# First loads, warm-up and one PSUM bank: six small changes at the start of a gated attention and FFN kernel

## The chip, the cores and the metric

The kernel runs on one core of one Trainium2 chip. The metric is the device time of one execution in microseconds (us); most kernels here were executed six times, and a change in time is judged against executions of the kernel before on the same chip in the same rounds. One execution of each kernel was traced. Its span (first to last instruction of the program) is about 1.25 us shorter than its device time. The traced execution of the kernel before took 288.19 us, less than any of the three executions that the prediction starts from.

## The reference

x is 2048 tokens of width 640 (bf16). Branch A is linear attention with 32 heads of width 20; branch B is a GEGLU feed-forward net of width 1728; a sigmoid gate mixes them.

```python
g = _sigmoid((x * gate_w).sum(-1, keepdims=True))
# A: q, k, v = x @ wqkv per head; pq = q @ w_phi, pk = k @ w_phi
#    phi = concat(softmax(p), softmax(-p)); kv = phi_k^T v; z = sum phi_k
#    a = ((phi_q @ kv) / (phi_q . z + 1e-6)) @ wo
# B: b = (gelu(x @ w_gate) * (x @ w_up)) @ w_down
return g * a + (1 - g) * b
```

## The kernel before

Everything that the change touches lies in the first 30 us. Loads are issued in program order, each engine on its own queue; a turned load (`dma_start_transpose`) brings x or a weight with its axes exchanged.

```python
    def loads(self):
        ...                                   # x: 4 tiles of 128 tokens in the first block
        sc.op("pool", ... memset gz ...)
        xload("sp", 0)                        # tiles 0, 1 (320 KB) on SyncE
        xload("act", 2)                       # tiles 2, 3 (320 KB) on ScalarE
        sc.dma("act", ... wphi_sb ...)        # 640 rows of 40 bytes
        for kt in range(KD):                  # V weight, five pieces of 160 KB
            sc.dma("sp", lambda e: e.dma_start(self.w3[:, kt, 0:D], w3[:, kt, 2 * D:3 * D]), writes=[("wv", kt)])
        sc.dma("act", ... gate_w into gz ...)
        xturn(4, 2)                           # tiles 4, 5 turned     } all on SyncE
        wload(self.wkT, D, "wkT")             # key weight turned     }
        xturn(6, 2)                           # tiles 6, 7 turned     }
        wload(self.wqT, 0, "wqT")             # query weight turned   }
        xturn(8, 4)
        xturn(12, 4)
        ...                                   # FFN weights, then masks on GpSimd

    def x_transpose(self, t, b, ek):          # five 128x128 transposes on TensorE into bank b,
        ...                                   # then one copy by ScalarE ("a") or VectorE ("d")

    def pq(self, b, i, n):                    # one query chunk
        bank = 6 + n % 2
        ...                                   # 5 matmuls, then exp(+) and exp(-) on ScalarE from that bank

    def attention_state(self):
        sc.op("dve", lambda e: e.memset(self.zero[:, :], 0.0), writes=["zero"])
        warm(7)                               # 7 matmuls of 512 columns on zeros, to wake the array
        xt(0, 6, "d"); xt(1, 7, "a"); xt(2, 2, "d"); xt(3, 3, "a")
        ...                                   # V projection of tiles 0-3, weight piece by weight piece
        self.v_early(4, 6); self.v_early(5, 0)          # needs tiles 4, 5
        f(0, "k", (2, 3), "d"); f(1, "k", (4, 5), "a")  # folds w_phi into the key weight: needs wkT
        self.v_early(6, 6)                              # needs tile 6
        ...                                             # f(0, "q", ...) needs wqT
        self.k_early(3, 0)                              # banks 0, 1
        self.k_norm(1)
        self.pq(0, 1, 1); self.pq(0, 0, 0); self.pq(0, 3, 3)   # banks 7, 6, 7
        self.gram(0)                                    # Gram product of tile 0
        ...
```

The softmax here doesn't subtract the row's maximum and nothing guards it: scores larger than these inputs give would overflow.

## Time and profile before

| | |
|---|---|
| device time | 288.81 us (288.63 to 288.95, 3 executions) |
| TensorE busy | 281.2 of 286.9 us |
| TensorE idle that the change aims at | the waits of the first 28.3 us |
| last wait of TensorE that matters | third query chunk, 0.34 us, until 28.34 us |

What it does not show is SyncE's queue, from the timeline of the first 12 us; columns are start, duration, engine ("SPq" is SyncE's queue of DMA issues), line, operation, operands and count.

```profile
0.79 0.41 SPq L217 DMA_DIRECT2D xtok<-in_A_x_dram  x1
1.27 2.30 SPq L234 DMA_DIRECT2D w<-in_A_wqkv_dram  x5
3.62 1.44 SPq L225 DMA_TRANSPOSE xT<-in_A_x_dram  x1
5.10 4.58 SPq L221 DMA_TRANSPOSE wkT<-in_A_wqkv_dram  x1
9.72 1.41 SPq L225 DMA_TRANSPOSE xT<-in_A_x_dram  x1
```

The durations are those of the issue, not of the transfer. The key weight (L221) holds the queue for 4.58 us, and tiles 6 and 7 can only be issued after it.

### The profile page before, as it was taken

What the parts mean: (1) busy time and instruction counts of PE and PEld (TensorE: products, weight loads), DVE (VectorE), ACT (ScalarE), POOL (GpSimd) and SP (SyncE); (2) the same over time, 40 slices, a digit from 0 to 9 for tenths busy, and PEclk for the clock granted to TensorE, in tenths of its full rate; (3) what the DMA queues carried; (4) which work ended last, traced back from release to release, by engine and by line L of the source; (5) the groups of instructions that cost most, each with busy time, mean ns of one, the idle gap of its engine ahead of it and who ended that gap; (6) DMA issues with size and microseconds to landing.
All of it is one profiled execution on the core that took longest, in us unless ns stands there. A gap on an engine that the chain in (4) does not pass through costs nothing.

```text
span 286.9 us, 7006 instructions
## 1 busy us (share of the span) xinstructions
PE 281.2 (98%) x3017; PEld 185.5 (65%) x3032; DVE 174.7 (61%) x353; ACT 105.0 (37%) x199; POOL 5.3 (2%) x36
## 2 busy tenths in 40 slices
PE   8999999999999999999999999999999999999996
PEld 3666689999994444444444444445777777777785
DVE  3248999999977553567242334225883883883801
ACT  3367887677663322322323223221112112112111
POOL 7000000000000000000000000000000000000000
PEclk9999999999999999999999999999999999999999
DMA  8999995000002000011000000000232333422221
GB/s 226 206 187 247 367 367 174 0 2 2 2 0 48 0 0 0 3 24 23 2 0 0 0 2 0 0 2 0 25 94 62 35 48 92 49 49 85 56 72 48
DMA packets 36937, 18.67 MB, mean 65 GB/s; under 512 B 28970, under 2 KB 36394, under 8 KB 36906
## 3 DMA queue, kind: packets, MB, share of 16 engines
q1 hardware_dynamic: 36096, 17.86, 26.1%
q8 instruction: 24, 0.39, 0.6%
q10 hardware_dynamic: 810, 0.35, 0.5%
q14 instruction: 7, 0.06, 0.1%
HBM read 9.04 MB, written 2.62 MB: 41 GB/s over the span
## 4 chain that ended last, share of the span: by engine, by line
PE 93%; SPq 3%; DMA 2%; ACT 1%; issue 1%; ACTq 0%
PE ps L352 60%; PE ps L714 28%; PE ps L658 2%; DMA xT<-in_A_x_dram 2%; PE ps L450 2%; SPq L221 2%; PE ps L332 1%; SPq L234 1%; SPq L225 1%; ACT Ek L414 0%; ACT Eq L519 0%; SPq L217 0%; ACT outsb L727 0%; ACT gcol L417 0%; ACTq L42 0%
## 5 line engine op out<-in xcount | busy, mean ns | idle before, releaser
L352 PE MATMUL ps<-xT,wg_sb 128*128 128x512 bf16 (+1 forms) x265 | 63.8, 379 | 0.4 <-issue 0.2
L352 PE MATMUL ps<-xT,wu_sb 128*128 128x512 bf16 (+1 forms) x263 | 63.3, 379 | 0.5 <-DVE hT L632 0.2
L630 ACT ACTIVATE gl<-ps 128x512 bf16<-128x512 f32 x52 | 30.9, 596 | 73.1 <-PE ps L352 68.7
L632 DVE TENSOR_TENSOR hT<-ps,gl 128x512 bf16<-128x512 f32 x39 | 26.7, 690 | 38.6 <-PE ps L352 38.5
L714 PE MATMUL ps<-wd_sb,hT 64*128 64x320 bf16 x648 | 49.5, 296 | 0.0
L352 PEld LDWEIGHTS ps<-xT,wu_sb 128*128 128x128 bf16 (+1 forms) x270 | 26.5, 99 | 29.8 <-DVE hT L632 0.5
L352 PEld LDWEIGHTS ps<-xT,wg_sb 128*128 128x128 bf16 (+1 forms) x270 | 26.2, 99 | 29.0 <-ACT gl L630 0.2
L352 PE MATMUL ps<-w,xT 128*64 128x512 bf16 (+6 forms) x398 | 41.6, 325 | 0.4 <-DMA xT<-in_A_x_dram 0.2
L727 ACT ACTIVATE outsb<-ps,Gm 128x320 bf16<-128x320 f32 (+2 forms) x31 | 14.5, 515 | 72.4 <-PE ps L714 72.4
L352 PEld LDWEIGHTS ps<-w,xT 128*64 128x64 bf16 (+1 forms) x400 | 35.8, 107 | 5.1 <-DMA xT<-in_A_x_dram 0.4
L714 PEld LDWEIGHTS ps<-wd_sb,hT 64*128 64x128 bf16 x648 | 31.0, 94 | 12.1 <-issue 0.4
L714 PE MATMUL ps<-wo_sb,goT 64*128 64x320 bf16 (+2 forms) x340 | 27.8, 288 | 0.0
L352 PE MATMUL ps<-xT,wq 128*64 128x512 bf16 (+1 forms) x184 | 26.1, 381 | 0.4 <-ACT Eq L519 0.3
L434 DVE TENSOR_TENSOR Ek<-Ek,Dk 128x640 bf16<-128x640 bf16 x32 | 25.0, 822 | 0.6
L685 DVE TENSOR_TENSOR O<-ps,RH 128x640 bf16<-128x640 f32 x32 | 24.8, 816 | 0.0
L425 DVE TENSOR_REDUCE Dk<-Ek 128x64 f32<-128x1280 bf16 x16 | 23.7, 1479 | 0.1
L519 ACT ACTIVATE Eq<-ps 128x512 bf16<-128x512 f32 x40 | 21.7, 605 | 1.1 <-PE ps L352 0.8
L414 ACT ACTIVATE Ek<-ps 128x640 bf16<-128x640 f32 x32 | 20.7, 703 | 3.6 <-PE ps L352 3.6
L632 DVE TENSOR_TENSOR xT<-ps,gl 128x512 bf16<-128x512 f32 x13 | 9.0, 691 | 18.2 <-PE ps L352 18.2
L714 PEld LDWEIGHTS ps<-wo_sb,goT 64*128 64x128 bf16 x340 | 16.1, 94 | 5.4
L352 PEld LDWEIGHTS ps<-xT,wq 128*64 128x64 bf16 (+1 forms) x185 | 15.3, 109 | 3.4 <-ACT Eq L519 0.8
L714 PE MATMUL ps<-wd_sb,xT 64*128 64x320 bf16 (+2 forms) x270 | 16.7, 269 | 0.0
(69 smaller groups left out, 173.2 us busy)
## 6 DMA issues: line engine op xcount, KB each, us to landing
out_dram<-outsb SPq DMA_DIRECT2D x7, 320.0 KB, 2.3
wd_sb<-in_B_w_down_dram SPq DMA_DIRECT2D x1, 2080.0 KB, 14.3
wg_sb<-in_B_w_gate_dram SPq DMA_DIRECT2D x1, 1120.0 KB, 5.7
wu_sb<-in_B_w_up_dram SPq DMA_DIRECT2D x1, 1120.0 KB, 8.2
wg_sb<-in_B_w_gate_dram SPq DMA_DIRECT2D x1, 960.0 KB, 9.8
wu_sb<-in_B_w_up_dram SPq DMA_DIRECT2D x1, 960.0 KB, 10.4
w<-in_A_wqkv_dram SPq DMA_DIRECT2D x5, 160.0 KB, 4.7
wo_sb<-in_A_wo_dram SPq DMA_DIRECT2D x1, 800.0 KB, 9.7
```

The costliest lines, as they stand in the source:

```text
L221: sc.dma("sp", lambda e: e.dma_start_transpose(T[:, :, :], self.wqkv[:, c0:c0 + D]), writes=[key])
L352: self.sc.op("pe", lambda e: e.matmul(self.ps[a:z, bank * 512 + c0:bank * 512 + c0 + n], lhs[:, a:z], rhs, start=first, stop=fin), reads=r ...
L414: self.sc.op("act", lambda e, s=s, scale=scale: e.activation(self.Ek[:, se, s, :], self.ps[:, o:o + self.D], AF.Exp, scale=scale), reads=[ ...
L425: sc.op("dve", lambda e: e.tensor_reduce(self.Dk[:, se, 0, :].rearrange("p (s h) -> p s h", h=H), self.Ek[:, se, :, :].rearrange("p s (h d ...
L434: sc.op("dve", lambda e, v=v, r=r: e.tensor_tensor(v, v, r, ALU.mult), reads=[("Rk", se)], writes=[("Ek", se, s)])
L450: sc.op("pe", lambda e: e.matmul(self.ps[a:a + 64, b * 512 + c:b * 512 + c + 2 * nf], va[:, lo:lo + 64], self.Ek[:, se, :, f0:f0 + nf], st ...
L519: sc.op("act", lambda e, s=s, scale=scale: e.activation(self.Eq[:, s, i, b * self.BT:(b + 1) * self.BT], self.bank(bank), AF.Exp, scale=sc ...
L630: sc.op("act", lambda e: e.activation(self.gl[:, slot, :], self.bank(banks[0]), AF.Gelu_apprx_tanh), reads=[("ps", banks[0])], writes=[("g ...
L632: sc.op("dve", lambda e: e.tensor_tensor(hT, self.bank(banks[1]), self.gl[:, slot, :], ALU.mult), reads=[("ps", banks[1]), ("gl", slot)], ...
L685: dve(lambda e, o=o, f=f, s=s: e.tensor_tensor(o, V[s][:, :, :, 0:DH], f, ALU.mult), rb + [key(6 + s)], [("O", s, sl)], guard=old)
L714: sc.op("pe", lambda e: e.matmul(self.bank(bk, w), lhs, rhs, start=opens and x == 0, stop=end and not opens, skip_group_check=True), reads ...
L727: sc.op("act", lambda e: e.activation(dst, self.bank(bk, w), AF.Copy, scale=g), reads=rd, writes=wr)
```

## The change

Two words first. TensorE's array starts "cold" (0.43 us from one 512-column matmul to the next) and is later "warm" (0.22 us). The "head" is everything up to the first query chunk, near 26 us.

The intent of the change: the first half of x should arrive earlier, undisturbed by the second half and by w_phi's many short rows; the warm-up should not wait for a memset; ScalarE's table should be loaded early; tile 3 should not wait for ScalarE's slower copy; and the third query chunk should not wait for bank 7.

```diff
@@ alloc @@
-        self.zero = T("zero", [P, 512], BF16)
         self.gz = T("gz", [P, P], BF16)
         self.gcol = T("gcol", [P, NT], F32)
         self.gtmp = T("gtmp", [P, NT], F32)
@@ -225,11 +224,17 @@
             sc.dma("sp", lambda e: e.dma_start_transpose(self.xT[:, :, a:z], self.x[a:z, :]),
                    writes=[("xT", k) for k in range(t, t + n)])
         sc.op("pool", lambda e: e.memset(self.gz[:, :], 0.0), writes=["gz"])
+        sc.op("act", lambda e: e.activation(self.gtmp[:, 0:1], self.nc.const_aps.tensor(1.0, [P, 1], BF16), AF.Exp),
+              writes=["gtmp"])
+        sc.op("pool", lambda e: e.memset(self.ident[:, :], 0.0), writes=["ident"])
+        sc.op("pool", lambda e: e.affine_select(self.ident[:, :], self.ident[:, :], pattern=[[-1, P]],
+                                                compare_op=ALU.not_equal, fill=1.0, base=0, channel_multiplier=1),
+              writes=["ident"])
         xload("sp", 0)
-        xload("act", 2)
+        xload("sp", 2)
         sc.dma("act", lambda e: e.dma_start(
             self.wphi_sb[:, :, :], self.wphi.rearrange("h d f -> (h d) f").rearrange("(i p) f -> p i f", p=P)),
-            writes=["wphi"])
+            reads=["ident"], writes=["wphi"])
         for kt in range(KD):
             sc.dma("sp", lambda e: e.dma_start(self.w3[:, kt, 0:D], w3[:, kt, 2 * D:3 * D]), writes=[("wv", kt)])
         sc.dma("act", lambda e: e.dma_start(self.gz[0:KD, :], self.gw.rearrange("(k p) -> k p", p=P)), writes=["gz"])
@@ -258,9 +263,6 @@
 
         def pool(fn, writes, reads=()):
             sc.op("pool", fn, reads=reads, writes=writes)
-        pool(lambda e: e.memset(self.ident[:, :], 0.0), ["ident"])
-        pool(lambda e: e.affine_select(self.ident[:, :], self.ident[:, :], pattern=[[-1, P]],
-                                       compare_op=ALU.not_equal, fill=1.0, base=0, channel_multiplier=1), ["ident"])
         for i in range(KD):
             n = self.HHI[i] - self.HLO[i] + 1
             base = P * i - DH * self.HLO[i]
@@ -509,9 +511,9 @@
                       writes=[("KV", i, r, g)])
                 self.kvk[i, r].append(("KV", i, r, g))
 
-    def pq(self, b, i, n):
-        sc = self.sc
-        bank = 6 + n % 2
+    def pq(self, b, i, n, bank=None):
+        sc = self.sc
+        bank = 6 + n % 2 if bank is None else bank
         for kt in range(self.KD):
             self.mm(bank, 0, 512, self.wq2[:, kt, i * P:(i + 1) * P], self.xT[:, kt, b * self.BT:(b + 1) * self.BT],
                     kt == 0, kt == self.KD - 1, [("xT", t) for t in range(4 * b, 4 * b + 4)] + [("wq2", kt)])
@@ -534,18 +536,15 @@
         NT = self.NT
         order = [(b, i) for b in range(self.NB) for i in range(self.KD)]
         sc = self.sc
-        sc.op("dve", lambda e: e.memset(self.zero[:, :], 0.0), writes=["zero"])
-
-        def warm(n):
-            for i in range(n):
-                sc.op("pe", lambda e: e.matmul(self.bank(0), self.zero[:, 0:P], self.zero[:, :], start=True, stop=True),
-                      reads=["zero"], writes=[("ps", 0)])
+        ones = self.nc.const_aps.tensor(1.0, [P, 512], BF16)
+        for n in (512, 512, 512, 512, 512, 512, 128):
+            sc.op("pe", lambda e: e.matmul(self.bank(0, n), ones[:, 0:P], ones[:, 0:n], start=True, stop=True),
+                  writes=[("ps", 0)])
         vs, ve, xt = self.v_step, self.v_first_evac, self.x_transpose
-        warm(7)
         xt(0, 6, "d")
         xt(1, 7, "a")
         xt(2, 2, "d")
-        xt(3, 3, "a")
+        xt(3, 3, "d")
         for t in range(4):
             vs(t, 0)
         for t in range(4):
@@ -585,7 +584,7 @@
         self.k_norm(1)
         self.pq(0, 1, 1)
         self.pq(0, 0, 0)
-        self.pq(0, 3, 3)
+        self.pq(0, 3, 3, 0)
         self.columns = True
         self.gram(0)
         self.k_norm(2)
```

## The prediction

> **What bounds the kernel now.** I read the page first: busy shares, then the strip of 40 slices.
>
> ```profile
> PE 281.2 (98%) x3017; PEld 185.5 (65%) x3032; DVE 174.7 (61%) x353; ACT 105.0 (37%) x199; POOL 5.3 (2%) x36
> PE   8999999999999999999999999999999999999996
> PEclk9999999999999999999999999999999999999999
> ```
>
> TensorE has work in hand for 281.2 of 286.9 us at the full granted clock, and only the first slice is short of 9 apart from the last. The change takes no matmul out of the stream except seven warm-up ones, of which it puts back six and a quarter. So all it can win is idle time of TensorE, and I listed that next, with the waits by length over the whole span and then the timeline of TensorE and its weight loads in the first 30 us. The rows that show a wait:
>
> ```profile
> 0.92 0.27 DVE L537 MEMSET zero<- 128x256 uint32 x1 [0.92 <-PEq L830]
> 1.24 3.17 PE L541 MATMUL ps<-zero 128*128 128x512 bf16 x7 [1.24 <-DVE zero L537]
> 4.28 1.12 PEld L291 LDWEIGHTS ps<-ident,xtok 128*128 128x128 bf16 x20 [0.78 <-DMA xtok<-in_A_x_dram]
> 5.81 0.39 PEld L364 LDWEIGHTS ps<-w,xT 128*128 128x128 bf16 x4 [0.30 <-ACT xT L297]
> 6.41 3.40 PEld L364 LDWEIGHTS ps<-w,xT 128*128 128x128 bf16 x26 [0.21 <-ACT xT L297]
> 14.80 1.36 PEld L352 LDWEIGHTS ps<-w,xT 128*128 128x128 bf16 x10 [0.36 <-DMA xT<-in_A_x_dram]
> 20.00 0.58 PEld L332 LDWEIGHTS ps<-BD,wqT 128*128 128x128 bf16 x11 [0.21 <-DMA wqT<-in_A_wqkv_dram]
> 28.34 1.25 PE L352 MATMUL ps<-xT,wq 128*128 128x512 bf16 x5 [0.34 <-ACT Eq L519]
> ```
>
> In order: warm-up behind a VectorE memset; transposes behind the load of x; V projection of the first block behind ScalarE's copies of transposed tiles 1 and 3; the V projection of tile 6 behind the turned load of x tiles 6 and 7; the first fold of the query weight behind the turned query weight; and the third query chunk behind ScalarE's exponentials. After 28.34 the same list over the rest of the span has only 0.2 us behind VectorE and 0.2 us of issue. So all that matters happens in the first 28 us, and what shift exists at 28.3 us reaches the end unchanged. Then the chain of waits for the first 40 us, to see which of these count:
>
> ```profile
> 3.62 1.44 SPq L225
> 5.10 4.58 SPq L221
> 9.72 5.04 DMA xT<-in_A_x_dram
> 14.76 0.05 issue
> 14.80 1.53 PE ps L352 x10
> ...
> 25.94 1.30 ACT Ek L414 x2
> 27.24 0.07 ACT gcol L417
> 27.30 0.99 ACT Eq L519 x2
> 28.29 0.05 issue
> 28.34 1.25 PE ps L352 x5
> ```
>
> The chain does not run through x's first load, the warm-up or the copies at all. Up to 14.76 it is SyncE's queue of DMA issues and the landing of x tiles 6 and 7. A saving on TensorE before 14.6 us therefore ends in a longer wait at 14.8, unless that landing comes earlier too. Only the ScalarE piece at 25.94 to 28.29 is on the chain and touched by the change.
>
> **What the Trainium skill says.** (1) "DMA: Bandwidth & Descriptors", Issuing engines are not separate DMA queues: DMAs of ScalarE and SyncE run on the same 16 DMA engines and interleave, and a second issuer saves only issue time. The trace agrees: the two halves of x, issued together at 0.79, landed 3.5 and 3.6 us later, both at about 4.3. (2) The same page, Queues, rings and completion order: each engine goes round the rings that have work, a packet at a time. That is why w_phi, on ScalarE's ring behind its half of x, moved only from about 3.7 us (686 packets of that queue in 3.7 to 4.9). With x gone from this ring it will be served as soon as it is issued, between x's packets. (3) "TensorE: Matmul & The Clock Gate", Part 1: about 3.4 us of activity wakes the array, a 512-column matmul taking 426.7 ns cold, 215.7 warm. The weight loads of the warm-up start at 1.65, 2.07, 2.50, 2.93 and 3.35, 0.43 apart, so cold; the 20 transposes from 4.28 take 1.29 in all, so warm. (4) "ScalarE activation tables: per-element evaluation and per-set limits", What a function is on this engine, puts one table load at 1283 ns; the trace has one of 1283 ns at 2.44 and one at the GELU.
>
> **The change part by part.**
> Warm-up: the memset and its wait go. The other engines start their own work at 0.79, so the first matmul can start near 0.85 rather than 1.24. Six of 0.427 and one of 0.107 are 2.67 us, ending near 3.5 rather than 4.23.
> x in turn: by the DMA windows the engines moved 0.65 MB by about 3.7 us, and both halves landed near 4.3, 0.55 us after. Served first, half one (0.33 MB) has moved by about 2.75 and lands near 3.3; tiles 0 and 1 are turned from about 3.5, perhaps still cold (10 x 0.107 = 1.07 at most), to 4.2 or 4.6. Half two, slowed a little by w_phi's packets, lands at 4.3 to 4.5, and tiles 2 and 3 take 10 x 0.057 = 0.57: V projection from about 5.1 rather than 5.42. The first piece of the V weight landed near 1.27 + 3.7 = 5.0, so earlier is not to be had. Gain there, 0.3.
> Tile 3's copy on VectorE: 492 ns there against 700 on ScalarE, and tile 1 is copied about 0.7 earlier, so the two waits of 0.30 and 0.21 mostly go. In the matmul row they are 4.56 us of stream against 16 x 0.27 = 4.34, so the gain is 0.2.
> Early exponential: moves the 1283 ns table load from 2.44 to 0.8. It was over at 3.72, before the first copy at 5.06: worth 0.
> w_phi: its wait for the identity (ready at 1.65) moves the issue from 1.24 to about 1.7. VectorE needs it at 5.74 and TensorE only at 13.8, so even a landing at 6 costs 0.
> Sum so far: TensorE is ready for tile 6 at 14.62 - 0.5 = 14.1. But tile 6 landed at 14.76. So this 0.5 is worth 0 unless the landing moves by d.
> The landing: SyncE has one more issue of 0.41 plus a gap, 0.46 in all, ahead of the five weight pieces and everything after. If issue set the pace, d = +0.46. The DMA windows say otherwise for most of it:
>
> ```profile
> 2.75:3.75 1.00, 1.00 (x3) 0.30 (x2) 0.00 (x0) 0.97 (x1) 0.77 (x6) 1.00 0.99 389
> 4.50:6.50 2.00, 2.00 (x27) 1.39 (x25) 1.66 (x6) 1.30 (x2) 1.72 (x14) 1.00 1.09 334
> 7.50:11.00 3.50, 3.50 (x28) 2.18 (x27) 0.47 (x2) 0.57 (x2) 0.00 (x0) 1.00 1.24 275
> ```
>
> The last two columns are the share of the 16 engines and GB/s: they are full from 2 to 6.5 us and again from 7.5 to 11, so bytes queue up behind the issues. The turned key weight took 4.58 us to issue for 640 rows, where 256 rows took 1.44: in proportion 3.60, so about 1.0 us of it was waiting for room. That slack is more than 0.46, and the bytes ahead are the same as before. I take d = 0, with +0.46 possible. The query weight, issued 5.87 us long, follows the same rule.
> Free bank: the third chunk waited for bank 7 until 28.29. Bank 0 was last read by the key exponentials of tile 3, done at 27.24, while TensorE gets there at 28.00. So the whole 0.34 of matmul idle goes. The next reader, the Gram product of tile 0, then comes at 29.19 rather than 29.52; VectorE is done with that tile at 28.99, so there is room, but only 0.2. ScalarE idles 0.33 in each later round, so it keeps up.
> Sum: 0 (head) + d (0) - 0.34 = -0.34, hence about 288.81 - 0.34 = 288.47; I say 288.45.
>
> **The rivals.**
> First, SyncE's issue order is the bound up to 14.8: each landing comes 0.46 later, the bank returns 0.34, and the time is 288.81 + 0.46 - 0.34 = 288.93. For it speaks the chain, which goes through these issues; against it the 1.0 us of slack in the key weight's issue. About one in five.
> Second, the landing comes earlier, because x no longer alternates with w_phi and V pieces, or a pause that the windows show at 6.5 to 7.5 (98 GB/s) shrinks. Then up to 0.5 of TensorE's head becomes real: 288.81 - 0.34 - 0.4 = about 288.1. About one in five.
> Third, the bank's gain is lost again at the Gram product or in bank 6, which the fourth chunk still needs. VectorE is busy from 25 to 50 us almost without a gap (3.58 us a tile against TensorE's 3.82), so lost TensorE time can't hide there but margins grow by 0.2 a tile. Then 288.8. One in ten.
> Fourth, the short warm-up ends before x arrives and the clock wakes late. Cold V projections would be bounded by the 0.5 of slack for the first microsecond; beyond that the time would rise to about 289. One in twenty.
>
> **Range and chances.** The likely outcomes run from 288.1 to 288.9, and the runs before scatter by 0.16 each way. I predict 288.45, and 287.95 to 288.9 for eight in ten. 2% is 5.8 us, while all idle of TensorE in the first 30 us is about 2 us by the windows (8.76, 9.64, 5.85 and 3.76 us busy in the stretches ending at 10, 20, 25.9 and 30): faster by over 2% gets 0.01, slower 0.01, within 0.98.
>
> **What would show it.** Warm-up matmuls from about 0.85 without a memset; the first transposes waiting near 3.5 and a second wait for x near 4.3; no row of the V projection waiting for ScalarE; the wait for x tiles 6 and 7 grown from 0.36 to about 0.9 with the matmul still at 14.8 (14.3 would be the second rival, 15.2 the first); no wait for ScalarE at the third query chunk; the Gram product of tile 0 about 0.3 earlier. A third chunk that still waits, or a new wait of the Gram product for VectorE, would prove the bank's term wrong.

## The result, and the profile after

Ratios here are the mean time of one kernel's fast executions over the mean of the other's from the same rounds, so not quite the ratio of the medians.

| kernel | median us | lowest to highest | ratio to before, 95% interval |
|---|---|---|---|
| before, same rounds | 288.72 | 288.10 to 288.95 (6) | |
| changed | 287.94 | 287.54 to 288.57 (6) | 0.9979 [0.9963, 0.9994] |
| before, a later call, other chip | 288.48 | 287.68 to 288.92 (11) | |
| changed, that call | 288.09 | 287.71 to 289.35 (6) | 0.9995 [0.9975, 1.0014] |

The means differ by 0.62 us in the first call and 0.11 in the second, 0.37 on average; the forecast was 0.36. The single executions of either kernel are spread over 0.8 to 1.6 us, so neither call alone fixes the gain to better than some 0.5 us.

The traced execution of the changed kernel took 288.29 us, a slow one among its six, with a span of 287.0 against 286.9 before: in this pair of traces nothing was won (the traced execution of the kernel before was a fast one). That is useful, because it shows what was won and lost on the way. First the busy time of the engines in four stretches, the kernel before and then the changed one (columns: stretch, its length, TensorE, weight loads, VectorE, ScalarE and GpSimd busy with instruction counts, granted clock, DMA share, GB/s):

```profile
0.00:10.00 10.00, 8.76 (x60) 4.62 (x61) 2.34 (x8) 2.58 (x3) 5.31 (x36) 1.00 0.93 231
25.90:30.00 4.10, 3.76 (x27) 1.63 (x28) 4.03 (x5) 3.69 (x8) 0.00 (x0) 1.00 1.01 376
```

```profile
0.00:10.00 10.00, 7.99 (x54) 4.52 (x55) 2.57 (x8) 2.19 (x3) 5.29 (x36) 1.00 0.92 217
25.90:30.00 4.10, 4.04 (x31) 2.00 (x31) 4.03 (x5) 3.79 (x10) 0.00 (x0) 1.00 0.99 354
```

TensorE's wait at the query chunk is gone (3.76 to 4.04 us busy in the last stretch), but the first 10 us hold 0.77 us less work than before. Now the timeline of TensorE in the changed kernel, to be laid beside the rows in the prediction:

```profile
0.83 2.83 PE L541 MATMUL ps<-const-bfloat16-1.0 128*128 128x512 bf16 x7 [0.83 <-PEq L829]
3.72 1.53 PE L293 MATMUL ps<-ident,xtok 128*128 128x128 bf16 x20
6.36 4.53 PE L366 MATMUL ps<-w,xT 128*128 128x480 bf16 x32 [1.11 <-DMA w<-in_A_wqkv_dram]
...
15.33 1.53 PE L354 MATMUL ps<-w,xT 128*128 128x512 bf16 x10
...
26.32 3.19 PE L354 MATMUL ps<-xT,wq 128*128 128x512 bf16 x14
29.52 0.46 PE L452 MATMUL ps<-Ek,vaug 128*64 128x120 bf16 x11
```

The warm-up starts 0.41 earlier and the transposes 0.57 earlier, as intended. But the V projection starts at 6.36 instead of 5.42, with a new wait of 1.11 us for the first piece of the V weight. Tile 6 is reached at 15.33 instead of 14.80. The three query chunks run through (x14, no wait), and the Gram product of tile 0 starts at 29.52, where it started before: what the loads lost, the bank gave back. SyncE's queue, same trace, against the five rows of before:

```profile
0.79 0.89 SPq L216 DMA_DIRECT2D xtok<-in_A_x_dram  x2
1.73 2.39 SPq L239 DMA_DIRECT2D w<-in_A_wqkv_dram  x5
4.16 1.86 SPq L224 DMA_TRANSPOSE xT<-in_A_x_dram  x1
6.06 4.18 SPq L220 DMA_TRANSPOSE wkT<-in_A_wqkv_dram  x1
10.29 1.40 SPq L224 DMA_TRANSPOSE xT<-in_A_x_dram  x1
```

The one more issue pushed the V weight from 1.27 to 1.73, the first turned load from 3.62 to 4.16 and tiles 6 and 7 from 9.72 to 10.29. They landed 5.0 us after that issue, at 15.29, where the kernel before had 14.76. And the chain of waits of the changed kernel:

```profile
1.73 4.50 DMA w<-in_A_wqkv_dram
6.22 0.14 issue
6.36 4.53 PE ps L366 x32
```

It runs no longer through the turned loads but through the first piece of the V weight, which took 4.50 us from issue to landing against 3.7 before. The two paths are nearly level here: tile 6 landed at 15.29, and its matmuls started at 15.33.

### The profile page after: what moved, and what is told of

Same layout as the page of the kernel before. It is cut to its first block, busy times and chain, and to the rows that moved or that the text cites. A ratio compares the mean times of both kernels' runs of the same rounds, so it can differ in the third digit from the quotient of the medians.

```text
span 287.0 us, 7005 instructions
## 1 busy us (share of the span) xinstructions
PE 280.9 (98%) x3017; PEld 185.7 (65%) x3032; DVE 174.9 (61%) x353; ACT 104.5 (36%) x199; POOL 5.3 (2%) x36
## 4 chain that ended last, share of the span: by engine, by line
PE 96%; DMA 2%; issue 1%; SPq 0%; ACT 0%
PE ps L354 61%; PE ps L713 28%; PE ps L657 2%; PE ps L366 2%; PE ps L452 2%; DMA w<-in_A_wqkv_dram 2%; PE ps L334 1%; SPq L216 0%; ACT outsb L726 0%; PE ps L316 0%
## 5 line engine op out<-in xcount | busy, mean ns | idle before, releaser
L354 PEld LDWEIGHTS ps<-xT,wq 128*64 128x64 bf16 (+1 forms) x185 | 15.3, 108 | 2.9
## 6 DMA issues: line engine op xcount, KB each, us to landing
wu_sb<-in_B_w_up_dram SPq DMA_DIRECT2D x1, 960.0 KB, 10.2
```

Source lines behind the costliest of these rows:

```text
L354: self.sc.op("pe", lambda e: e.matmul(self.ps[a:z, bank * 512 + c0:bank * 512 + c0 + n], lhs[:, a:z], rhs, start=first, stop=fin), reads=r ...
```

## The experiments

The theory after the traces: (a) the bank is worth what was predicted; (b) the changed loads are worth nothing or less, since the added issue on SyncE is handed on to tile 6 in full. The rivals: the loads do win in most executions and the traced one was unlucky; or it is the bytes, w_phi's short rows or the waking of the array that matter, not the issue. All twelve runs below gave a correct result.

### The changed kernel once more

> The changed kernel unaltered, once more, because its executions lie 1.0 us apart (287.54 to 288.57) and the one with a trace was among the slow ones (288.29). If the load timing of the head differs from one execution to the next, this trace will show another start of the V projection than 6.36 us (5.1 to 5.5 in a fast one) and the landing of the first V-weight piece will move with it. If 6.36 is what every execution has, and the gain is elsewhere, it stays at 6.2 to 6.5. Time: 0.6 us under the kernel before, 287.5 to 288.5.

Measured: 288.09 us median, ratio 0.9995 [0.9975, 1.0014]. The traced execution took 289.35. Its timeline:

```profile
3.93 2.31 PE L293 MATMUL ps<-ident,xtok 128*128 128x128 bf16 x20 [0.27 <-DMA xtok<-in_A_x_dram]
6.04 4.91 PE L366 MATMUL ps<-w,xT 128*128 128x480 bf16 x32
16.56 1.53 PE L354 MATMUL ps<-w,xT 128*128 128x512 bf16 x10 [1.12 <-DMA xT<-in_A_x_dram]
```

and the last pieces of its chain of waits ahead of tile 6:

```profile
4.11 2.47 SPq L224
6.58 0.05 issue
6.63 4.21 SPq L220
10.84 0.04 issue
10.88 5.63 DMA xT<-in_A_x_dram
```

The head does differ from execution to execution: here the V piece landed in time (4.0 us after issue), but all 20 transposes ran cold, 0.107 us apart (2.31 us in all against 1.29 in the kernel before), and tile 6 landed at 16.5. The start of the V projection was expected at 5.1 to 5.5 or at 6.2 to 6.5; it was 6.04, for a third reason.

### The bank alone, and all but the bank

```diff
-        self.pq(0, 3, 3)        # kernel before
+        self.pq(0, 3, 3, 0)     # bank_only: this line (and the argument of pq) alone
```

> The kernel before with only the third query chunk put in bank 0. Theory of the prediction: the wait of 0.34 us at that chunk goes and the time falls by 0.34 us (ratio 0.9988); the loads are untouched, so the V projection starts at 5.4 and tile 6 is still waited for at 14.8. Rival: the gain is lost again at the Gram product of tile 0 or at bank 6; then the ratio is 1.000.

Measured: 287.68 us median, ratio 0.9985 [0.9964, 1.0005]; in means 0.46 us under the kernel before.

```diff
-        self.pq(0, 3, 3, 0)     # changed kernel
+        self.pq(0, 3, 3)        # no_bank
```

> The changed kernel with the third query chunk back in bank 7. Theory of the prediction, as amended by the trace of the changed kernel: the head is worth nothing or loses (landings 0.4 to 0.5 us later), so this is 0 to 0.4 us slower than the kernel before. Rival: the head gives 0.3 us or more in most executions; then this is faster than the kernel before by that.

Measured: 288.59 us median, ratio 1.0019 [0.9991, 1.0046]; in means 0.58 us over the kernel before, 0.19 without one execution at 290.93. The rows of the query chunks, first with the bank alone, then with all but the bank:

```profile
26.17 3.19 PE L352 MATMUL ps<-xT,wq 128*128 128x512 bf16 x14
29.36 0.46 PE L450 MATMUL ps<-Ek,vaug 128*64 128x120 bf16 x11
```

```profile
26.95 2.11 PE L354 MATMUL ps<-xT,wq 128*128 128x512 bf16 x9
29.39 1.25 PE L354 MATMUL ps<-xT,wq 128*128 128x512 bf16 x5 [0.34 <-ACT Eq L521]
30.57 0.48 PE L452 MATMUL ps<-Ek,vaug 128*64 128x120 bf16 x11
```

From the start of the chunks to the Gram product it is 3.19 us with bank 0 and 3.62 with bank 7. In the kernel before it is 29.52 - 25.90 = 3.62, and in the changed one 29.52 - 26.32 = 3.20. The other traces agree: 3.62 to 3.63 in all three with bank 7, 3.19 in all eleven with bank 0. So the bank is worth 0.43 us in every trace. By the starts of single matmuls it saves 0.50 ahead of the third chunk (0.72 from the matmul before it with bank 7, 0.22 with bank 0) and gives 0.08 back at the Gram product, which starts 0.38 to 0.39 after the last matmul of the chunks with bank 0 and 0.31 with bank 7. Its weight load now waits for VectorE (the trace with the bank alone):

```profile
29.33 0.35 PEld L450 LDWEIGHTS ps<-Ek,vaug 128*64 128x64 bf16 x11 [0.47 <-DVE Ek L434]
```

So the rival (the gain lost at the Gram product) was right for 0.08 us and falls for the rest: from the start of the Gram product to the end of the last matmul it is 254.5 to 254.6 us in all 14 traces, so nothing more is lost on the way. From the last matmul to the end of the span it is another 2.4 to 3.0 us (2.85 and 2.46 in the two traces of the kernel before), so part of the scatter of the times comes after all matmuls. By the times alone the bank's gain is not clear of noise. The head alone is not shown to be faster by the times: its interval runs from 0.3 us faster to 1.3 us slower.

### The second half of x back on ScalarE's queue

```diff
-        xload("sp", 2)
+        xload("act", 2)
```

> The changed kernel with the second half of x back on ScalarE's queue, the rest as changed. If SyncE's order of issue paces the landings (first rival), the five V pieces are issued from 1.27 again and tile 6 lands at 14.8 instead of 15.3, and the time is 0.3 to 0.5 us under the changed kernel. If the bytes pace them, tile 6 lands at the same time in both kernels of this call within 0.2 us and the times agree within 0.2 us.

Measured: 288.92 us median, ratio 1.0012 [0.9984, 1.0039]. This one missed both expectations. The V pieces were issued from 1.27 again and the first turned load at 3.70, but the second piece landed 5.8 us after its issue, and tile 6 at 16.9:

```profile
5.44 1.39 PE L366 MATMUL ps<-w,xT 128*128 128x480 bf16 x8
7.57 3.45 PE L366 MATMUL ps<-w,xT 128*128 128x480 bf16 x24 [0.74 <-DMA w<-in_A_wqkv_dram]
```

So an early issue was not enough here: the V pieces ahead of the turned loads landed late, the last at 8.87 against 7.79 in the kernel before. Why they came so late here is open; w_phi, which landed at 7.8, is a suspect that the next runs did not convict.

### A second trace of the kernel before

> The kernel before unaltered, for a second trace of it: how far its own landings move from one execution to the next. If the chain of SyncE's issues is steady and only the change shifts it, tile 6 lands at 14.4 to 15.0 again and the key weight's issue ends at 9.7. If loads move by themselves as much as between the kernels, tile 6 lands after 15.3.

Measured: one execution, 288.07 us. The key weight's issue ended at 9.75 and tile 6 landed at 14.9, as in the first trace, so SyncE's chain was steady in these two. What differs is TensorE's own pace. Its chain of waits:

```profile
0.80 3.73 DMA xtok<-in_A_x_dram
4.53 0.05 issue
4.58 1.76 PE ps L291 x20
6.33 4.56 PE ps L364 x32
```

Here the first tiles of x landed later (4.53 against 4.24), the first half of the transposes ran cold, the V projection started at 6.17 and TensorE reached tile 6 at 15.22, after it had landed. So in the kernel before, too, the landing at 14.8 binds only in some executions. My prediction took one trace for the rule.

### The V weight in two loads instead of five

```diff
-        for kt in range(KD):
-            sc.dma("sp", ... self.w3[:, kt, 0:D] ...)
+        for lo, hi in ((0, 1), (1, KD)):
+            sc.dma("sp", ... self.w3[:, lo:hi, 0:D] ...)
```

> The changed kernel with the V weight in two loads (the first piece alone, the other four in one) in place of five: the same bytes, three issues of 0.47 us fewer on SyncE ahead of the turned loads, whose issue starts near 2.7 us instead of 4.1. If SyncE's issue paces the turned loads, the key weight's issue ends about 1.4 us earlier (near 8.8) and tile 6 lands near 14; TensorE is then not held at tile 6 and the time is 0.4 to 1.0 us under the changed kernel. If the bytes pace them, the key weight's issue still ends at 10.2 or later and the time is that of the changed kernel within 0.2.

Measured: 289.65 us median, ratio 1.0051 [1.0028, 1.0074], the slowest run. (Only this one and the next have an interval that lies above 1.)

```profile
2.67 1.97 SPq L224 DMA_TRANSPOSE xT<-in_A_x_dram  x1
4.69 6.08 SPq L220 DMA_TRANSPOSE wkT<-in_A_wqkv_dram  x1
```

```profile
8.88 3.45 PE L367 MATMUL ps<-w,xT 128*128 128x480 bf16 x24 [2.19 <-DMA w<-in_A_wqkv_dram]
```

The turned load was issued 1.4 us earlier and gained nothing: the key weight's issue only took longer (6.08 us) and ended at 10.77. So the pure issue theory falls as well. The slowdown has another cause that the last row shows: the matmuls of the second piece wait until all four pieces have landed, at 8.8.

### w_phi after everything of the first block

```diff
-        sc.dma("act", ... wphi_sb ..., reads=["ident"], writes=["wphi"])     # in loads()
+        sc.dma("act", ... wphi_sb ..., writes=["wphi"])                      # after xt(1, 7, "a")
```

> The changed kernel with w_phi issued after ScalarE's copy of tile 1 (about 5.4 us) instead of at 1.69, so that its 640 short rows run behind the first V-weight piece. If they hold that piece up, it lands near 5.0 to 5.2 instead of 5.7 to 6.2, the V projection starts at 5.1 to 5.5, and the other pieces land up to 1 us earlier (6.0 for the second). If not, the first piece still lands after 5.6. The time falls only if tile 6 lands earlier as well: by 0 to 0.5 us.

Measured: 288.94 us median, ratio 1.0024 [1.0005, 1.0042]. w_phi was issued at 4.96. The first V piece landed 3.4 us after its issue, at 5.1, against 6.2 and 5.7 in the two traces of the changed kernel, and the V projection started at 5.32. That is as expected if w_phi had held it up, but the same piece landed at 5.1 to 5.4 in three other kernels with w_phi in its changed place, so the run does not settle it. Tile 6 landed at 15.5. The time is 0.1 to 1.2 us above the kernel before by its interval; the traced execution (288.07) is the fastest of its six, so it doesn't show why.

### A longer warm-up

```diff
-        for n in (512, 512, 512, 512, 512, 512, 128):
+        for n in (512,) * 8:
```

> The changed kernel with eight warm-up matmuls of 512 columns (to about 4.3 us) instead of six and one of 128 (to 3.5). If the short warm-up leaves the array cold in some executions (the second trace of the changed kernel had all 20 transposes at 0.107 us), the transposes here run at 0.056 and the V projection starts by 5.5, and no execution shows a mean granted clock under 0.998. If the array wakes by a clock of its own whatever the warm-up is, 0.107 appears here too. Time against the changed kernel: within 0.3 us, as tile 6 is waited for later.

Measured: 288.04 us median, ratio 1.0002 [0.9974, 1.0030].

```profile
0.84 3.57 PE L541 MATMUL ps<-const-bfloat16-1.0 128*128 128x512 bf16 x8 [0.84 <-PEq L829]
4.20 2.31 PE L293 MATMUL ps<-ident,xtok 128*128 128x128 bf16 x20
```

TensorE worked without a break from 0.84, and still all 20 transposes ran cold. So in this execution the longer warm-up did not wake the array sooner. In the traces taken together the starts of single matmuls change from cold to warm spacing between 4.2 and 7.0 us.

### One more issue without bytes

```diff
+        sc.dma("sp", lambda e: e.dma_start(self.spare[:, :], self.x[0:P, 0:32]), writes=["spare"])   # 8 KB, never read
         xturn(4, 2)
```

This is added to the kernel before, with the bank change.

> The kernel before with the bank change, and one more load on SyncE, of 8 KB that nobody reads, between the V weight and the first turned load: one more issue of 0.43 to 0.47 us and hardly a byte, nothing else of the changed head. In the nine traces of this call's chips so far the first turned load lands at its issue + 5.1 to 5.3 us or at the last V piece + 1.2, whichever is later, the key weight's issue ends 0.6 to 1.1 after that landing and tile 6 lands 4.6 to 5.7 later. Theory (issue and landing latency in a chain): the first turned load is issued from 4.2, lands near 9.4 instead of 8.9, the key weight's issue ends near 10.2 instead of 9.7 and tile 6 lands at 15.0 to 15.5 instead of 14.4 to 14.9. Rival (bytes, as the prediction had it): 9.7 and 14.4 to 14.9 as without it. Time: 0 to 0.4 us over the bank change alone, so 0.4 under to level with the kernel before.

Measured: 288.28 us median, ratio 0.9987 [0.9968, 1.0006].

```profile
4.23 2.23 SPq L226 DMA_TRANSPOSE xT<-in_A_x_dram  x1
6.51 3.75 SPq L222 DMA_TRANSPOSE wkT<-in_A_wqkv_dram  x1
10.30 1.40 SPq L226 DMA_TRANSPOSE xT<-in_A_x_dram  x1
```

This is the test that the prediction's main step needed. With one more issue of 0.43 us the key weight's issue ended at 10.26, against 9.7 to 9.8 in the three traces without it, and tile 6 landed at 15.6 (5.3 after 10.30), against 14.4 to 14.9. Bytes do not explain it: there are hardly any more, and the last V piece landed at 7.80, as in the first trace of the kernel before (7.79). Nor does the landing of the first turned load: at 9.10 it came 0.1 to 0.3 later than in those three, while the end of the issue moved by 0.5. It is one trace. In this execution it cost nothing, since x itself landed late (4.9) and the array woke late, so that TensorE reached tile 6 only at 16.02. The time agrees: it is not shown to be slower than the bank alone.

### Tiles 4 to 7 in one turned load

```diff
-        xturn(4, 2)
+        xturn(4, 4)
         wload(self.wkT, D, "wkT")
-        xturn(6, 2)
```

Three bases: the kernel before with the bank change, the changed kernel, and a mixture (x on two queues and w_phi as before, no early exponential; early warm-up, VectorE's copy of tile 3 and the bank as changed).

> The kernel before with the bank change and with x tiles 4 to 7 turned in one load ahead of the key weight in place of two loads around it. Theory: the landing that held TensorE at tile 6 (14.4 to 14.9) is gone, tiles 4 to 7 land near 9.5 to 10.3 (needed at 11.1), the key weight near 13.5 (needed at 13.8 to 14.4), and the query weight follows it sooner. TensorE's own pace sets the start at tile 6 (14.6 to 15.2 with the array woken at 4.3 to 5.5), so the time is 0.3 to 0.6 us under the kernel before, as with the bank alone, with less scatter. Rival: the longer turned load lands after 11.1 or pushes the key weight past 14.4, a new wait as long as the old one.

Measured: 288.36 us median, ratio 0.9999 [0.9980, 1.0019].

> The changed kernel with the same merged turned load. If tile 6's landing (15.3 to 16.5 there) is what takes the head's gain away, it now starts by TensorE's pace (14.0 to 15.0), and the time falls by 0.5 to 1.3 us under the changed kernel and 0.6 to 1.2 under the kernel before. If the head is slow for another reason (V pieces late, array cold), the time stays as it was.

Measured: 289.06 us median, ratio 1.0019 [0.9997, 1.0041].

```profile
11.62 2.66 PE L353 MATMUL ps<-w,xT 128*128 128x512 bf16 x19 [0.26 <-DMA xT<-in_A_x_dram]
16.12 0.80 PE L333 MATMUL ps<-BD,wkT 128*128 128x140 bf16 x12 [1.83 <-DMA wkT<-in_A_wqkv_dram]
```

> A candidate to beat both: merged turned load and bank change, x in halves on two queues and w_phi as in the kernel before (so no added issue on SyncE), but the early warm-up on the constant and VectorE's copy of tile 3. Expected 0.6 to 1.0 us under the kernel before: tile 6 at 14.2 to 14.8, no wait for its landing. Against it: the warm-up ends at 3.5, x lands at 4.3 to 4.5, and the array may wake late.

Measured: 288.79 us median, ratio 1.0005 [0.9980, 1.0031]. The fold of the key weight waits 1.24 us for its landing there, and the V projection starts at 5.86 with half of the transposes cold.

The rival named for these runs was right: the merged load holds SyncE for 4.5 to 4.8 us, the key weight is issued at 8.5 to 8.7 and lands at 14.9 to 16.1 instead of 12.3 to 13.5. TensorE waits at the fold instead of at tile 6, clearly so in two of the three. No candidate beat both kernels.

### What the traces say together

Times in us from the start of the span; "landed" is issue start plus time to landing.

| trace | first turned load issued, landed | key weight's issue ends | tile 6 landed | TensorE starts tile 6 | V projection starts |
|---|---|---|---|---|---|
| before | 3.6, 9.0 | 9.7 | 14.8 | 14.80 | 5.42 |
| before again | 3.8, 8.9 | 9.8 | 14.9 | 15.22 | 6.17 |
| bank alone | 3.7, 9.0 | 9.7 | 14.4 | 15.03 | 5.98 |
| one more issue | 4.2, 9.1 | 10.3 | 15.6 | 16.02 | 7.01 |
| changed | 4.2, 9.4 | 10.2 | 15.3 | 15.33 | 6.36 |
| changed again | 4.1, 9.7 | 10.8 | 16.5 | 16.56 | 6.04 |
| all but the bank | 4.1, 9.3 | 10.4 | 15.9 | 15.96 | 5.47 |
| longer warm-up | 4.1, 9.5 | 10.5 | 15.5 | 15.59 | 6.34 |
| w_phi late | 4.1, 9.6 | 10.2 | 15.5 | 15.60 | 5.32 |
| x on ScalarE | 3.7, 10.1 | 10.8 | 16.9 | 16.93 | 5.44 |
| V weight in two | 2.7, 10.0 | 10.8 | 15.4 | 16.66 | 5.30 |

In all eleven the key weight's issue ends 0.6 to 1.2 us after the first turned load has landed, and tile 6 lands 4.6 to 6.1 after that. The first turned load lands at least 4.9 us after its issue and at least 1.2 after the last V piece. Where the first turned load was issued at 4.1 or later, tile 6 landed at 15.3 or later (six of six); with 3.6 to 3.8 and V pieces in time, at 14.4 to 14.9 (three of three). The added issue without bytes is one of the six.

The ends of the key weight's issue fit another pair of bounds more closely than that landing. The issues of the first turned load and of the key weight never took less than 6.0 us together, however they shared it (1.44 and 4.58 in the first trace of the kernel before, 2.53 and 3.43 in the second), and they never ended less than 1.9 us after the landing of the last V piece. In ten of the eleven traces the end is within 0.4 us of the later of these two bounds; in the changed kernel's second trace it is 0.7 after it. This was fitted afterwards and not tested. Whether the landing, the issue itself or something else holds the key weight back is not shown.

## Why the prediction was right or wrong

The time came out as forecast by ratio (0.9988 expected; 0.9979 and 0.9995 measured, both intervals contain it). In absolute terms the median of 287.94 lies at the lower edge of the range, 0.01 below 287.95, in rounds in which the kernel before was 0.09 below its earlier median. That it fits so well is in part luck: the bank returned more than forecast, two steps for the head were wrong to the slow side, and the scatter hides what they cost.

- **The bank: right, and undersized.** 0.34 predicted, 0.43 in the traces. The room at the Gram product, put at 0.2, was too large: its weight load did wait for VectorE, which the prediction had named as the sign that the bank's term is wrong. That cost 0.08 of the 0.50 saved at the chunk.
- **The landing of tile 6: this is the step that failed.** "I take d = 0, with +0.46 possible." It was +0.53 in the first trace and 0.5 to 1.8 in the five traces of kernels with x in turn and the V weight in five pieces, against 14.76. The reasoning behind it was that about 1.0 us of the key weight's 4.58 us of issue "was waiting for room" and that this slack would absorb 0.46. The traces show no such slack: the two turned loads were issued from 4.16 instead of 3.62, and the key weight's issue ended at 10.24 instead of 9.68. A proportion to 1.44 us is no measure of it either, since the other trace of the kernel before shares the same 6.0 us as 2.53 and 3.43. A wait absorbs a delay only if what ends it does not move.
- **The V projection "from about 5.1": wrong in all three traces with this head.** It started at 6.36 and 6.04 in the two traces of the changed kernel and at 5.47 in that of all but the bank. The step assumed that the first V piece lands near 5.0, although the prediction itself puts 0.46 us more of issue ahead of it. In the first trace it landed 4.5 us after the later issue. The waits for ScalarE's copy at tiles 1 and 3 did go, and the gain was swallowed.
- **x in turn: half right.** Half one landed at 3.7 (3.3 predicted), half two at 4.5 (4.3 to 4.5 predicted).
- **w_phi: wrong order, right verdict.** It was to be served "as soon as it is issued". The DMA view of the changed kernel has, for 3.5 to 4.0 us and then for 4.0 to 4.5, on ScalarE's queue (packets, MB, share of the engines):

```profile
q10 hardware_dynamic: 4, 0.00, 0.5%
```

```profile
q10 hardware_dynamic: 264, 0.01, 36.2%
```

So its rows moved from 4.0 us, 2.3 us after the issue at 1.69, no earlier than in the kernel before, and landed at 7.5 rather than by 6. VectorE waited 1.6 us for it at the block diagonal, and nobody waited for VectorE.
- **The early exponential and the warm-up: as predicted** (table load at 0.79, first matmul at 0.83). Neither was tested alone, so what they are worth is not shown.
- **The head as a whole: predicted 0, and not shown to differ from it.** All but the bank measured 1.0019 [0.9991, 1.0046]. In the traces it is later: the first query chunk starts at 25.90 to 26.20 in the three with the old head and at 26.32 to 27.55 in the three with the new one. That a later landing of 0.5 us and more costs so little is explained in part by what the prediction did not know: the kernel before is not always held at tile 6 either (15.22 and 15.03 by its own pace in two traces of three). How much the head costs on average stays open; the executions are too scattered for these runs to say.

Of the rivals, the first (SyncE's order, 288.93) was right about the landing and wrong in its time. The third was right for 0.08 us. The fourth (the array wakes late) happened as well, in traces of the kernel before and of the changed one. The executions at 290.93 (all but the bank), 291.49 (V weight in two) and 290.39 (longer warm-up) had a mean granted clock of 0.994 against 0.999 to 1.000 of the others; none of them was traced, so what lowered it is open.

## What to carry to other kernels

A PSUM bank that is already free removes a wait for nothing, and the gain is seen in every trace: look for such waits first, and then at what waits next, since part of the gain can be lost there. Before you count a wait as slack that can absorb a delay, find what ends the wait and ask whether that moves too; in a DMA queue with turned loads in a row, bytes alone did not tell when the next one lands. And where single executions differ by 1 us, one trace shows one path: take a second trace of the kernel before, before you say what binds it.

## What the Trainium skill lacked or had wrong

- "DMA: Bandwidth & Descriptors", Issuing engines are not separate DMA queues: a second issuer saves only issue time, "usually small relative to the DMA itself". An issue of 0.43 us is small beside the 4.6 to 5.3 us that the load three issues later took, but that load landed 0.7 to 1.3 us later with it (15.6 in one trace, 14.4 to 14.9 in three without).
- The same page, DMA Transpose (X-bar), gives rules for transposes from different queues but does not say how transposes in a row on one queue follow each other: in eleven traces the issue of the second ended 0.6 to 1.2 us after the landing of the first, and 0.33 MB landed 4.6 to 6.1 us after its issue.
- The same page, Queues, rings and completion order, has the engines go round the rings that have work. w_phi, issued at 1.69 on a ring of its own, had moved 4 packets by 4.0 us. No page says what held it here.
- "TensorE: Matmul & The Clock Gate", Part 1, puts the waking about 4 us into activity, within 500 ns from run to run, with a free-running window. The scatter here is wider: the spacing changed at 4.2 to 7.0 us, some 3 to 6 us after first matmuls at 0.84 or 1.25. No run here tests the window.
- No page was found that says how far executions of one unchanged kernel scatter: 287.68 to 288.92 us for the kernel before in one call. The traces show part of it in the first loads and part after the last matmul (2.4 to 3.0 us).
